# Layer-norm output of an adaLN + attention + FFN block: transposed and scaled by chunks of features instead of tiles of tokens, with a new opening order and a new issue order on every engine

## The chip, the cores and the metric

The kernel runs on one core of one Trainium2 chip. Its time is the device time of one execution in microseconds (us). An engine is one of PE (TensorE: matmuls and transposes), ACT (ScalarE), DVE (VectorE) and POOL (GpSimd); SP (SyncE) issues nearly all DMAs. Each engine runs its own instructions strictly in the order in which they were written, and waits at an instruction until its operands are there.

## The reference

```python
x = A_x                                     # 2048 tokens x 512 features
mod = (silu(c) @ w_mod).reshape(1, 6, 1, 512)   # sa, ca, ga, sb, cb, gb
h = layernorm(x) * (1 + ca) + sa
x = x + ga * A(h)      # q, k, v = h @ wq, h @ wk, h @ wv; 32 heads of 16;
                       # 4 segments of 512 tokens: masked softmax inside a segment,
                       # plus a memory (phi(k)^T v, summed over earlier segments); then @ wo
h = layernorm(x) * (1 + cb) + sb
x = x + gb * (relu(h @ w1 + b1) ** 2 @ w2 + b2)  # 1792 hidden features
```

All in float32. Matrices are 512 features wide, so four 128-row chunks.

## The kernel before, in words

Products of float32 accuracy are made of three products of rounded operands (type `fp32r`): every operand is split into a high half (`hi`, a cast on ACT) and a low half (`lo`, value minus `hi`, a subtraction on DVE or POOL), and hi*hi + hi*lo + lo*hi are summed.

The attention part works on four segments `s` of 512 tokens, each in four units `u = 4s + cc` of eight heads. What the change touches is the way from `x` to the projections of a segment:

- `load_x` brings four tiles `xt` of 128 tokens x 512 features; `ln_stats`, `ln_rstd` and `ln_apply` normalise them (DVE and POOL).
- `ln_transposed` turns one tile on PE (`ln_turn`, four 128x128 transposes into one PSUM bank `blnq`, L610). Each quarter of the bank is one chunk `k` of 128 features, and it has its own scale and bias (`modc`), so `ln_affine` (L616 on ACT, L618 on DVE) applies them in pieces of 128x128: in segment 0 two pieces on ACT and two on DVE for each tile, later four on ACT. `ln_split` (L623) then casts the tile into `HT[:, 0]` and writes the low half into `HT[:, 1]`.
- `HT` is one buffer, 128 features x (hi, lo) x 4 chunks x 512 tokens. `qk(u)` (Q and K of a unit) and `vproj(s)` (V of the segment) read all of it; both wait for all four tiles (`HTN[s]`), and a tile of the next segment waits for every user of the segment before (`HUSE[s - 1]`). The sum over the four chunks is made on half-height arrays, first the upper and lower 64 rows one way (turn 0), then crossed (turn 1), with a tiny ACT instruction (`fence`, L767) between. Unit 0 is the exception: full-height matmuls (L785 to L787) on two halves of 256 tokens.
- `qk` ends with the halves of Q and K in `sg`, and 12 DMAs (`fill`, L845) spread them into the slots `ST` of the scores. `clear` (L717) sets the unused rows of `ST` once from `pad`, six DMAs of 256 KB.
- `a_quad` computes scores (`ba`, L900) of which DVE takes the row maxima (L905, 512 of them with an accumulator read each); `b_quad` computes them again, shifted by the maxima, exponentiates on ACT (`pt`, L1073), masks on POOL (L1060), multiplies with V (`bpv`, L1115).

At the start the scale and bias themselves must be made: `silu(c)` (`crow`, `cs`), two products with `wmod` (`bmod`, L567, for `ca` and `sa`), a copy `t`, and a turn into columns (`bmodc`, L589). Meanwhile the weights are split: `split_w` casts on ACT (L701) and subtracts on POOL (L705; one piece on DVE). `N_WARM` products of the identity with itself (`bwarm`, L539), of which each is two instructions in the trace, fill PE before the first real work.

After the attention come the output projection (`wo_tile`) and the FFN (`bh` L1485, `bpf` L1547 to L1549).

The order on every engine is written out by hand: `ORDER` holds for each engine a list of node numbers, which a planner (`Plan.run`) follows; nodes not in a list follow by priority. The planner assigns buffers; waits come from the real dependences.

## Time and profile before

| | us |
|---|---|
| median of 3 runs (lowest, highest) | 761.86 (759.72, 762.55) |
| the profiled execution: time, span | 762.53, 760.8 |
| busy in the span: PE, DVE, ACT, POOL | 749.1, 604.0, 414.3, 300.7 |
| first real projection (`bqk`, unit 0) starts | 23.74 |
| first score matmul (`ba`) starts | 40.30 |
| first FFN matmul (`bh`), about | 443.1 |

The span is the time from the first to the last recorded event on the core; the execution's time is 1.7 us longer. The granted clock of PE is 0.997 over the span. A busy PE in such a profile can also be a PE between two matmuls, since their ends are modelled, so PE's work is read from how matmuls follow each other.

### The profile page before, as it was taken

What the parts mean: (1) busy time and instruction counts of PE and PEld (TensorE: products, weight loads), DVE (VectorE), ACT (ScalarE), POOL (GpSimd) and SP (SyncE); (2) the same over time, 40 slices, a digit from 0 to 9 for tenths busy, and PEclk for the clock granted to TensorE, in tenths of its full rate; (3) what the DMA queues carried; (4) which work ended last, traced back from release to release, by engine and by line L of the source; (5) the groups of instructions that cost most, each with busy time, mean ns of one, the idle gap of its engine ahead of it and who ended that gap; (6) DMA issues with size and microseconds to landing.
All of it is one profiled execution on the core that took longest, in us unless ns stands there. A gap on an engine that the chain in (4) does not pass through costs nothing.

```text
span 760.8 us, 18140 instructions
## 1 busy us (share of the span) xinstructions
PE 749.1 (98%) x6649; PEld 608.1 (80%) x6649; DVE 604.0 (79%) x1815; ACT 414.3 (54%) x937; POOL 300.7 (40%) x368
## 2 busy tenths in 40 slices
PE   9999999999999999999999999999999999999997
PEld 8987677666787768876666689998999898988986
DVE  5788889999899899999999877868866764666543
ACT  2668777898867987678665844546112321221110
POOL 5676657667677695544241632251010020000000
PEclk9999999999999999999999999999999999999999
DMA  9787574544564345458733157653555345656521
GB/s 308 217 266 223 151 209 126 143 137 120 171 192 100 86 118 156 132 143 247 230 95 127 31 180 273 233 201 140 194 192 210 128 163 208 220 172 217 194 98 69
DMA packets 61058, 129.66 MB, mean 170 GB/s; under 512 B 8613, under 2 KB 23977, under 8 KB 59178
## 3 DMA queue, kind: packets, MB, share of 16 engines
q1 hardware_dynamic: 60818, 128.37, 53.4%
q8 instruction: 53, 0.87, 0.5%
q14 instruction: 35, 0.29, 0.1%
q10 hardware_dynamic: 152, 0.13, 0.1%
HBM read 81.29 MB, written 20.19 MB: 133 GB/s over the span
## 4 chain that ended last, share of the span: by engine, by line
PE 88%; DMA 4%; DVE 2%; ACT 2%; issue 1%; POOL 1%; SPq 1%; DVEq 0%; ACTq 0%; POOLq 0%
PE bh L1485 18%; PE bqk L793 9%; PE bpv L1115 8%; PE bpf L1548 7%; PE bpf L1547 7%; PE bpf L1549 7%; PE bv L866 6%; PE bpb L1056 6%; PE ba L900 6%; PE bwop L1217 2%; PE bwarm L539 2%; PE bwop L1218 2%; PE bwop L1219 2%; PE blnq L610 2%; ACT pt L1073 1%
## 5 line engine op out<-in xcount | busy, mean ns | idle before, releaser
L905 DVE CUSTOM_DVE_ANT_0 ba<-ba,msk 128x384 f32<-128x384 f32 (+3 forms) x512 | 244.4, 511 | 21.0 <-PE ba L900 11.9
L1073 ACT ACTIVATE pt<-bpb 128x512 f32<-128x512 f32 x320 | 171.1, 611 | 28.4 <-PE bpb L1056 25.9
L1060 POOL TENSOR_SCALAR_AFFINE_SELECT pt<-pt 128x512 f32<-128x512 f32 x128 | 80.0, 646 | 91.8 <-ACT pt L1073 70.9
L793 PE MATMUL bqk<-HT,WQK 64*128 64x512 f32 x720 | 106.5, 398 | 0.1
L1056 PE MATMUL bpb<-ST 64*128 64x256 f32 (+2 forms) x512 | 80.2, 349 | 1.7 <-ACT oraw L1139 0.9
L1115 PE MATMUL bpv<-pt,VT 128*32 128x512 f32 (+3 forms) x1024 | 80.8, 440 | 0.7 <-POOL pt L1060 0.2
L793 PEld LDWEIGHTS bqk<-HT,WQK 64*128 64x128 f32 x720 | 74.6, 185 | 8.0 <-issue 1.2
L900 PE MATMUL ba<-ST 63*128 63x256 f32 (+2 forms) x512 | 79.5, 344 | 1.0 <-ACT pt L1073 0.7
L905 DVE DVE_READ_ACCUMULATOR2_ANT mx<- 128x1 f32 x512 | 72.3, 141 | 0.1
L900 PEld LDWEIGHTS ba<-ST 63*128 63x128 f32 x512 | 54.9, 186 | 21.7 <-ACT pt L1073 4.7
L1056 PEld LDWEIGHTS bpb<-ST 64*128 64x128 f32 x512 | 53.9, 186 | 19.4 <-issue 4.5
L1529 ACT CAST ST<-xx 128x512 fp32r<-128x512 f32 x41 | 25.2, 620 | 74.3 <-DVE xx L1521 60.6
L1485 PEld LDWEIGHTS bh<-ST 128*128 128x128 f32 x420 | 56.5, 190 | 3.6
L1485 PE MATMUL bh<-ST 128*128 128x256 f32 x420 | 58.9, 282 | 0.0
L1485 PE MATMUL bh<-ST,w 128*128 128x256 f32 x420 | 58.2, 282 | 0.0
L1485 PEld LDWEIGHTS bh<-ST,w 128*128 128x128 f32 x420 | 55.4, 190 | 2.6
L866 PE MATMUL bv<-WVO,HT 64*128 64x512 f32 x384 | 55.5, 395 | 0.0
L1115 PEld LDWEIGHTS bpv<-pt,VT 128*32 128x32 f32 x1024 | 27.8, 109 | 32.2 <-issue 25.1
L745 POOL TENSOR_TENSOR X1L<-X1L 128x512 fp32r<-128x512 f32 (+1 forms) x28 | 32.1, 1147 | 45.3 <-ACT X1L L744 45.1
L1547 PE MATMUL bpf<-w,ST 128*128 128x512 f32 x124 | 48.9, 395 | 0.0
L1548 PE MATMUL bpf<-w,ST 128*128 128x512 f32 x124 | 48.9, 395 | 0.0
L1549 PE MATMUL bpf<-w,ST 128*128 128x512 f32 x124 | 48.5, 391 | 0.0
(208 smaller groups left out, 1531.9 us busy)
## 6 DMA issues: line engine op xcount, KB each, us to landing
ST<-w1d SPq DMA_DIRECT2D x14, 1792.0 KB
w<-w1d SPq DMA_DIRECT2D x14, 1792.0 KB
ST<-sg SPq DMA_DIRECT2D x192, 128.0 KB
w1d<-X1L SPq DMA_DIRECT2D x21, 512.0 KB
xt<-in_A_x SPq DMA_DIRECT2D x16, 256.0 KB
wm<-in_w_mod SPq DMA_DIRECT2D x16, 256.0 KB
xw<-in_A_x SPq DMA_DIRECT2D x16, 256.0 KB
X1L<-in_B_w SPq DMA_DIRECT2D x7, 512.0 KB
```

Of the source, the lines that this page charges most:

```text
L793: nc.tensor.matmul(bank(banks[w]), W3(w, k, x, cols.start, cols.stop)[r], HT[r, y, k], start=turn == k == i == 0, stop=turn == 1 and k == ...
L866: nc.tensor.matmul(bank(banks[t]), HT[r, x, k, (t2 + t) * P:(t2 + t + 1) * P], WVO[r, k, y], start=turn == k == i == 0, stop=turn == 1 and ...
L900: nc.tensor.matmul(dst[:, c0:c0 + n], ST[b:b + 63, 0, sl, qt * P:(qt + 1) * P], ST[b:b + 63, 1, sl, :n], start=True, stop=True)
L905: nc.vector.tensor_tensor_reduce(i, i, msk[:, 512 - n:], scale=1.0, scalar=-3e38, op0=ALU.add, op1=ALU.max, accum_out=o)
L1056: nc.tensor.matmul(dst, ST[b:b + 64, 1, sl, kb * P:(kb + 1) * P], ST[b:b + 64, 0, sl, q0:512], start=True, stop=True)
L1060: nc.gpsimd.affine_select(out=ap, in_=ap, pattern=[[0, ap.shape[1]], [1, P]], compare_op=ALU.is_ge, fill=0.0, base=0, channel_multiplier=-1)
L1073: ns = [op("ACT", 0.49, lambda j=j: nc.scalar.activation(buf("PPP"[n], pt)[:, i + j], bank(keys[j]), AF.Exp, scale=0.25), pr[slot] + 0.01 ...
L1115: nc.tensor.matmul(bank(o)[32 * hq:32 * hq + 32, q0:q0 + src.shape[1]], v[:, a:a + 32], src, start=start, stop=stop, tile_position=(0, 32 ...
L1485: nc.tensor.matmul(pb(i), A[:, x, kk], B[:, y, kk], start=kk == j == 0, stop=kk == 1 and j == 2)
L1547: nc.tensor.matmul(q, rh, wh, start=(i == 0), stop=False)
L1548: nc.tensor.matmul(q, rh, wl, start=False, stop=False)
L1549: nc.tensor.matmul(q, rl, wh, start=False, stop=(i == NF - 1))
```

## The change

- `ln_chunk` takes the place of `ln_transposed`: for each chunk `k` of features the four tiles are turned into one bank, so that a bank holds one chunk of all 512 tokens, and one instruction of 128x512 applies the scale and bias (in segment 0 chunks 0 and 2 on ACT, 1 and 3 on DVE; later all on ACT). The cast and the subtraction are per chunk too. All four tiles must be normalised before the first transpose.
- `qk` and `vproj` wait for the chunk that each step reads (`HTK`), not for the whole of `HT`, and a chunk of the next segment waits for the last readers of that chunk (`HKUSE`). `chunk` lets the direction alternate, so that the chunk that is free first is filled first and read first.
- Unit 0 is no longer done in two halves of 256 tokens: 24 matmuls of 128x512 in place of 48 of 128x256.
- `N_WARM` is 40 in place of 70.
- `ORDER` is new throughout, on all five engines. Instructions that are neither fillers nor of the way above are the same in kind and number: ACT has 14 instructions of 128x512 for `lnf` in place of 56 of 128x128, DVE 2 in place of 8.

```diff
@@ -31,7 +31,7 @@
-N_WARM = 70
+N_WARM = 40
...
@@ -55,169 +55,168 @@
 ORDER = {
     "PE": """
-8-40 105 111 41 3 42-44 94 86 96 45 88 46-48 117 49 123 50-72 290-291 73-74 292 75-76 293 77 280-282 294 283-284 295
...
+8-24 3 25-35 56 36-39 58 64 78 82 40 66 90 41-42 86 43-47 252 246-247 253 248 254 249 255 401-404 291-292 406 293 407
...
@@ -609,33 +608,26 @@
-    def ln_affine(eng, f, q, sc, bi):
...
-    def ln_split(dst, t, f, low):
...
-    def ln_transposed(s, t, src, dst, pool, sc, bi, pr, after, put, wait=(), low="DVE", kind="#D"):
-
-        b = ("lnq", sc, s, t)
-        f = ("lnf", sc, s, t)
-        n = pe("F", 0.357, lambda: ln_turn(bank(b), src()), pr, after=after, get=[(kind, b)] + ([(pool, f)] if pool != "xr" else []),
-               put=put)
-        if low == "POOL":
-            af = [op("ACT", 1.38, lambda: ln_affine("av", buf(pool, f), bank(b), sc, bi), pr + 0.01, after=[n, *MODC[sc]], put=[b])]
+    def ln_chunk(s, k, pr, applied, wait):
+
+        b, f = ("lnq", s, k), ("lnf", s, k)
+        keys = [("xt", 4 * s + t) for t in range(4)]
+
+        def turn():
+            for t in range(4):
+                nc.tensor.transpose(bank(b)[:, t * P:(t + 1) * P], TL[keys[t]][:, k * P:(k + 1) * P], ident)
+        n = pe("F", 0.357, turn, pr, after=applied, get=[("#D" if s else "#A", b), ("oraw", f)], put=keys)
+        sc, bi = modc[:, CA, k:k + 1], modc[:, SA, k:k + 1]
+        if s or k % 2 == 0:
+            n = act(512, lambda: nc.scalar.activation(buf("oraw", f), bank(b), AF.Identity, scale=sc, bias=bi), pr + 0.01,
+                    after=[n, *MODC[CA]], put=[b])
         else:
-            af = [op("ACT", 0.69, lambda: ln_affine("a", buf(pool, f), bank(b), sc, bi), pr + 0.01, after=[n, *MODC[sc]], put=[b]),
-                  None]
-            af[1] = op("DVE", 0.64, lambda: ln_affine("v", buf(pool, f), bank(b), sc, bi), pr + 0.01, after=[af[0]], put=[b])
-        h = act(512, lambda: ln_split(dst(), t, TL[f], low)[0](), pr + 0.02, sbuf=True, after=[*af, *wait], put=[f])
-        l = op(low, 1.24 if low == "POOL" else 0.6, lambda: ln_split(dst(), t, TL[f], low)[1](), pr + 0.03, after=[h], put=[f], lock=True)
+            n = dve(512, lambda: nc.vector.tensor_scalar(buf("oraw", f), bank(b), sc, bi, op0=ALU.mult, op1=ALU.add), pr + 0.01,
+                    after=[n, *MODC[CA]], put=[b])
+        eng, e = (nc.gpsimd, "POOL") if s else (nc.vector, "DVE")
+        h = act(512, lambda: nc.scalar.copy(HT[:, 0, k], TL[f]), pr + 0.02, sbuf=True, after=[n, *wait], put=[f])
+        l = op(e, 1.24 if s else 0.6, lambda: eng.tensor_tensor(HT[:, 1, k], TL[f], HT[:, 0, k].bitcast(F32), op=ALU.subtract), pr + 0.03,
+               after=[h], put=[f], lock=True)
         return [h, l]
@@ -655,6 +647,11 @@
+    HTK, HKUSE = {}, {s: [[] for _ in range(KD)] for s in range(-1, NS)}
+
+    def chunk(s, turn, i):
+
@@ -668,13 +665,13 @@
-        HTN[s] = []
-        for t in range(4):
-            g = 4 * s + t
-            a = op("DVE", 0.48, lambda t=t, g=g: ln_apply(TL["xt", g], TL["xt", g], TL[mv][:, t]), p_turn[t] - 0.1,
-                   after=[r[t // n]], put=[mv, ("xt", g)], lock=True)
-            HTN[s] += ln_transposed(s, t, lambda g=g: TL["xt", g], lambda: HT, ("phi0", "phi1", "phi1", "oraw")[t] if s == 0 else "oraw", CA, SA, p_turn[t], [a],
-                                    [("xt", g)], HUSE[s - 1], "POOL" if s else "DVE", "#D" if s else "#A")
+        ap = [op("DVE", 0.48, lambda g=g, t=t: ln_apply(TL["xt", g], TL["xt", g], TL[mv][:, t]), p_turn[t] - 0.1,
+                 after=[r[t // n]], put=[mv, ("xt", g)], lock=True) for t, g in enumerate(range(4 * s, 4 * s + 4))]
+        HTK[s] = {}
+        for i in range(KD):
+            k = chunk(s, 0, i)
+            HTK[s][k] = ln_chunk(s, k, p_turn[i], ap, HKUSE[s - 1][k])
+        HTN[s] = [q for k in range(KD) for q in HTK[s][k]]
@@ -779,49 +776,44 @@
-        def mm(w, k, c):
-            p = bank(banks[w])
+        def mm(w, k):
             wh, wl = W3(w, k, 0, cols.start, cols.stop), W3(w, k, 1, cols.start, cols.stop)
-            nc.tensor.matmul(p[:, c], wh, HT[:, 0, k, c], start=(k == 0), stop=False)
-            nc.tensor.matmul(p[:, c], wh, HT[:, 1, k, c], start=False, stop=False)
-            nc.tensor.matmul(p[:, c], wl, HT[:, 0, k, c], start=False, stop=(k == KD - 1))
-
-        def half(turn, k):
+            for x, y, i in ((wh, 0, 0), (wh, 1, 1), (wl, 0, 2)):
+                nc.tensor.matmul(bank(banks[w]), x, HT[:, y, k], start=k == i == 0, stop=k == KD - 1 and i == 2)
+
+        def half(turn, k, first, last):
             for i, (x, y) in enumerate(((0, 0), (0, 1), (1, 0))):
                 for j in (1, 0) if turn else (0, 1):
                     w, r = j ^ turn, slice(64 * j, 64 * j + 64)
-                    nc.tensor.matmul(bank(banks[w]), W3(w, k, x, cols.start, cols.stop)[r], HT[r, y, k], start=turn == k == i == 0,
-                                     stop=turn == 1 and k == 0 and i == 2)
+                    nc.tensor.matmul(bank(banks[w]), W3(w, k, x, cols.start, cols.stop)[r], HT[r, y, k], start=first and i == 0,
+                                     stop=last and i == 2)
         done = {}
         if u:
             n = None
             for turn in (0, 1):
-                for k in range(KD):
-                    if turn and not k:
-                        n = fence(HT[64:65, 0, KD - 1, :1], pr[0] + 0.01, n)
-                    n = pe("R", 0.697, lambda turn=turn, k=k: half(turn, KD - 1 - k if turn else k), pr[turn] + 0.002 * k,
-                           after=[n] if n else [*HTN[s], *(z for w in (0, 1) for z in (WN[w, cc] if s == 0 else []))],
-                           get=() if turn or k else [("#D", b) for b in banks])
-                    if k == 0:
+                for i in range(KD):
+                    k = chunk(s, turn, i)
+                    if turn and not i:
+                        n = fence(HT[64:65, 0, k, :1], pr[0] + 0.01, n)
+                    n = pe("R", 0.697, lambda turn=turn, k=k, i=i: half(turn, k, turn == i == 0, turn == 1 and i == KD - 1), pr[turn] + 0.002 * i,
+                           after=[n, *(HTK[s][k] if not turn else ()),
+                                  *(z for w in (0, 1) for z in (WN[w, cc] if s == turn == i == 0 else []))],
+                           get=() if turn or i else [("#D", b) for b in banks])
+                    if i == 0:
                         HUSE[s].append(n)
+                    if turn:
+                        HKUSE[s][k].append(n)
                 HUSE[s].append(n)
             done[0] = done[1] = n
         for w in (0, 1):
             b = banks[w]
-            ends = []
-            for i in range(0 if u else 2):
-                c = slice(i * L // 2, (i + 1) * L // 2)
-                ht = HTN[s][4 * i:4 * i + 4]
-                n = None
-                for k in range(KD):
-                    n = pe("F", 0.35, lambda w=w, k=k, c=c: mm(w, k, c), pr[w] + 0.002 * k + 0.2 * i,
-                           after=[n] if k else [*ht, *(WN[w, cc] if s == 0 else []), *ends, *([] if u or i or w else [n_w0])], get=() if k or i else [("#D", b)])
-                    if k == 0:
-                        HUSE[s].append(n)
+            for k in range(0 if u else KD):
+                n = done[w] = pe("F", 0.697, lambda w=w, k=k: mm(w, k), pr[w] + 0.002 * k,
+                                 after=[done.get(w), *HTK[0][k], *(WN[w, cc] if k == 0 else []), *([] if k or w else [n_w0])],
+                                 get=() if k else [("#D", b)])
                 HUSE[s].append(n)
-                ends.append(n)
-                done[w] = n
+                HKUSE[s][k].append(n)
@@ -873,12 +865,16 @@
             n = None
             for turn in (0, 1):
-                for k in range(KD):
-                    if turn and not k:
-                        n = fence(WVO[64:65, KD - 1, 0, :1], pr[t2] + 0.01, n)
-                    n = pe("R", 0.697, lambda turn=turn, k=k, mm=mm: mm(turn, KD - 1 - k if turn else k), pr[t2 + turn] + 0.002 * k,
-                           after=[n] if n else [*HTN[s], *([z for c_ in range(4) for z in WN[2, c_]] if s == 0 else [])],
-                           get=() if turn or k else [("#D", b) for b in banks])
+                for i in range(KD):
+                    k = chunk(s, turn, i)
+                    if turn and not i:
+                        n = fence(WVO[64:65, k, 0, :1], pr[t2] + 0.01, n)
+                    n = pe("R", 0.697, lambda turn=turn, k=k, i=i, mm=mm: mm(turn, k, turn == i == 0, turn == 1 and i == KD - 1), pr[t2 + turn] + 0.002 * i,
+                           after=[n, *(HTK[s][k] if not turn else ()),
+                                  *([z for c_ in range(4) for z in WN[2, c_]] if s == turn == i == 0 else [])],
+                           get=() if turn or i else [("#D", b) for b in banks])
+                    if turn:
+                        HKUSE[s][k].append(n)
```

Three places of the order, before and after. PE from its first instruction to unit 0's first projection, before:

```order
L539 MATMUL bwarm<-ident 128x128 x33
L610 MATMUL blnq<-ident,xt 128x128 x8
L539 MATMUL bwarm<-ident 128x128
L529 MATMUL bcs<-ident,crow 128x4
L539 MATMUL bwarm<-ident 128x128 x3
L567 MATMUL bmod<-wmod,cs 32x512 x8
L589 MATMUL bmodc<-selc,t 128x1 x4
...
L610 MATMUL blnq<-ident,xt 128x128 x4
L539 MATMUL bwarm<-ident 128x128 x23
L785 MATMUL bqk<-HT,WQK 128x256
```

and in the change:

```order
L538 MATMUL bwarm<-ident 128x128 x17
L528 MATMUL bcs<-ident,crow 128x4
L538 MATMUL bwarm<-ident 128x128 x11
L566 MATMUL bmod<-wmod,cs 32x512 x4
L538 MATMUL bwarm<-ident 128x128 x4
L588 MATMUL bmodc<-selc,t 128x1 x4
L566 MATMUL bmod<-wmod,cs 32x512 x4
L618 MATMUL blnq<-ident,xt 128x128 x8
...
L618 MATMUL blnq<-ident,xt 128x128 x4
L538 MATMUL bwarm<-ident 128x128 x5
L782 MATMUL bqk<-HT,WQK 128x512 x24
```

The product for `ca` now stands by itself ahead of that for `sa`, the transposes stand behind both, and 5 fillers in place of 23 stand ahead of the first projection. In both versions fillers stand between some of the rows; before, they also stand inside unit 0's projections.

SP's DMAs from the start, before:

```order
L648 DMA xt<-in_A_x 128x512 x4
L552 DMA wmod<-in_w_mod 128x512 x8
L691 DMA w<-in_A_wk 128x4x128
L691 DMA w<-in_A_wk 128x4x384
L691 DMA X1L<-in_A_wq 128x4x128
L691 DMA X1L<-in_A_wq 128x4x384
L691 DMA w<-in_A_wv 128x4x128
L717 DMA ST<-pad 32x4x512 x4
L691 DMA w<-in_A_wv 128x4x384
```

and in the change:

```order
L551 DMA wmod<-in_w_mod 128x512
L640 DMA xt<-in_A_x 128x512 x3
L551 DMA wmod<-in_w_mod 128x512 x3
L640 DMA xt<-in_A_x 128x512
L551 DMA wmod<-in_w_mod 128x512 x4
L688 DMA X1L<-in_A_wq 128x4x128
L688 DMA w<-in_A_wk 128x4x128
L688 DMA w<-in_A_wk 128x4x384
L688 DMA w<-in_A_wv 128x4x128
L688 DMA X1L<-in_A_wq 128x4x384
L688 DMA w<-in_A_wv 128x4x384
L714 DMA ST<-pad 32x4x512 x2
```

The first pieces of `wq` and `wk` are ahead of the rest of the weights, and four of the six `pad` DMAs have moved behind the first fills: two stand behind 17 fills, two behind 31.

ACT where `HT` passes to segment 2 (with the buffers' numbers), before:

```order
L616 ACTIVATE lnf_2934<-blnq_2913,modc_79 128x128 x4
L1008 COPY pk_2958<-bpkt_2941 128x4x64
L1008 COPY pk_2958<-bpkt_2939 128x4x64
L744 CAST X1L_67<-X1L_67 128x512
L1073 ACTIVATE pt_2975<-bpb_2964 128x512
L1073 ACTIVATE pt_2975<-bpb_2965 128x512
L616 ACTIVATE lnf_2987<-blnq_2980,modc_79 128x128 x4
```

and in the change:

```order
L1069 ACTIVATE pt_2464<-bpb_2528 128x512
L622 ACTIVATE lnf_2564<-blnq_2552,modc_79 128x512
L622 ACTIVATE lnf_2573<-blnq_2566,modc_79 128x512
L622 ACTIVATE lnf_2582<-blnq_2558,modc_79 128x512
L764 CAST HT_65<-HT_65 1x1
L1004 COPY pk_2613<-bpkt_2595 128x4x64
L741 CAST X1L_67<-X1L_67 128x512
```

Three instructions of 128x512, for three chunks, stand together where two tiles' eight of 128x128 stood apart, around two exponentials (`pt`); the fourth chunk follows later.

305 lines of the change are left out of this document (147 added, 158 removed), and 16 rows, old and new, of the table ORDER.

## Prediction

> **What bounds the kernel now.** I read the page first, then the windows by stage, the timeline of the opening, and at last the waits. The page gives the totals:
>
> ```profile
> span 760.8 us, 18140 instructions
> PE 749.1 (98%) x6649; PEld 608.1 (80%) x6649; DVE 604.0 (79%) x1815; ACT 414.3 (54%) x937; POOL 300.7 (40%) x368
> ```
>
> PE at 98% says little by itself, since fillers count as busy. The windows tell the stages apart (busy us of PE, PEld, DVE, ACT, POOL, then clock, DMA share, GB/s): the attention from the first score to the first FFN matmul, the FFN, and the last stretch ahead of the first score.
>
> ```profile
> 41.30:443.10 401.80, 396.84 (x4365) 291.80 (x4364) 367.53 (x1345) 304.59 (x721) 238.65 (x296) 1.00 0.53 151
> 443.10:757.00 313.90, 312.86 (x1961) 280.68 (x1959) 210.92 (x421) 90.02 (x176) 39.20 (x32) 1.00 0.52 183
> 30.80:40.30 9.50, 9.50 (x81) 7.67 (x80) 7.13 (x16) 3.60 (x8) 5.71 (x7) 1.00 0.67 186
> ```
>
> In the attention DVE works 367.5 of 401.8 us (91%): it is the engine that sets the pace, with PE close behind. In the FFN PE works 312.9 of 313.9 and DVE only 210.9. Ahead of the first score DVE works 7.1 of 9.5 us, and before that PE waits, as the next rows show. So the kernel is a start of 41 us, a stretch at DVE's pace, and a stretch at PE's. What is saved ahead of the first score moves everything behind it. The start on PE:
>
> ```profile
> 1.90 9.01 PE L539 MATMUL bwarm<-ident 128*128 128x128 f32 x66 [1.90 <-POOL ident masks.py:199]
> 10.75 1.04 PE L610 MATMUL blnq<-ident,xt 128*128 128x128 f32 x8
> 12.96 1.92 PE L567 MATMUL bmod<-wmod,cs 128*32 128x512 f32 x16
> 16.03 0.95 PE L589 MATMUL bmodc<-selc,t 128*128 128x1 f32 x8
> 18.69 5.30 PE L539 MATMUL bwarm<-ident 128*128 128x128 f32 x46
> 23.74 0.37 PE L785 MATMUL bqk<-HT,WQK 128*128 128x256 f32 x1
> 30.77 3.01 PE L793 MATMUL bqk<-HT,WQK 64*128 64x512 f32 x24
> 39.28 1.09 PE L610 MATMUL blnq<-ident,xt 128*128 128x128 f32 x8
> 40.30 0.51 PE L900 MATMUL ba<-ST 63*128 63x256 f32 x4
> ```
>
> From 18.69 to 23.74 PE does nothing but fillers: it waits for the chain scale and bias, `lnf`, `HT`. That chain on ACT and DVE:
>
> ```profile
> 17.66 2.19 ACT L616 ACTIVATE lnf<-blnq,modc 128x128 f32<-128x128 f32 x6
> 21.17 1.14 ACT L623 CAST HT<-lnf 128x512 fp32r<-128x512 f32 x2
> 17.02 0.16 DVE L591 TENSOR_SCALAR modc<-bmodc 128x4 f32<-128x4 f32 x1 [0.96 <-PE bmodc L589]
> 21.91 1.29 DVE L623 TENSOR_TENSOR HT<-lnf,HT 128x512 fp32r<-128x512 f32 x2
> 24.57 2.39 DVE L623 TENSOR_TENSOR HT<-lnf,HT 128x512 fp32r<-128x512 f32 x2 [0.74 <-ACT HT L623]
> 25.14 1.27 POOL L705 TENSOR_TENSOR WQK<-w,WQK 128x512 fp32r<-128x512 f32 x1 [4.81 <-ACT WQK L701]
> ```
>
> The scale and bias are there at 17.18, the first low halves at 23.2, and the last at 26.96: ten us for four tiles.
>
> **The opening, part by part.** When do the loads land? The transfer rates in slices of 1 us, and one wait that a landing ended:
>
> ```profile
> GB/s 0 18 230 350 299 289 352 369 363 361 373 357 370 364 343 342 369 343 359 331 257 277 312 246 96 115 375 402 406 262 37 0 33 172 203 129 110 346 386 281
> 16.62 0.62 ACT L701 CAST WQK<-X1L 128x512 fp32r<-128x512 f32 x1 [1.01 <-DMA X1L<-in_A_wq]
> ```
>
> Twelve loads of 256 KB (262 KB of 1000 bytes; `x`, then both `wmod`) are 3146 KB, which the rates reach at 11.4; `bmod` starts at 12.96. Up to the first piece of `wq` it is 4456 KB, reached at 15.05; ACT starts at 16.62. Both lag by 1.56 us, so I take landing = bytes moved + 1.56. In the change the last tile of `x` is load 8 (2097 KB, 8.5 + 1.56 = 10.1), `ca`'s weights are complete with load 7 (9.4), `sa`'s with load 12 as before (12.96), the first piece of `wq` follows (13.7).
>
> The tokens become the later branch: the fourth tile must have its statistics, `rstd`, and all four their scaling ahead of any transpose. The nearest rows:
>
> ```profile
> 9.95 0.69 DVE L597 BATCH_NORM_STATS2 bs<-xt 128x6 f32<-128x512 f32 x1
> 10.94 0.22 POOL L602 TENSOR_SCALAR mv<-mv 128x2 f32<-128x2 f32 x1 [1.95 <-DVE mv L598]
> 11.24 0.71 POOL L603 TENSOR_TENSOR mv<-mv,nhalf 128x2 f32<-128x2 f32 x1
> 11.99 1.00 DVE L606 TENSOR_SCALAR xt<-xt,mv 128x512 f32<-128x512 f32 x2 [1.14 <-POOL mv L603]
> ```
>
> From the start of the statistics to the first scaling is 2.04 us: 10.1 + 2.0 = 12.1. Four scalings at 0.46 with one `modc` (0.16) between end at 14.2. Eight transposes take 0.87 (10.75 to the next row at 11.62), a filler 0.22: `bmodc` starts at 15.3, `modc` is there 1.15 later (16.03 to 17.18): 16.45, against 17.18. Now four chunks, not four tiles with four pieces each. ACT does chunk 0 and its cast (0.6 each, ending 17.75), DVE chunks 1 and 3 in the meantime (0.61 each, to 17.8), then the low half of chunk 0 (0.7): 18.5. Unit 0 starts at about **18.55, against 23.74**. Chunk 1 follows in time; chunk 2 stands last on ACT and DVE (cast 19.95, low half 20.7), so the third step waits 0.8. Four steps a matrix at 0.70 (three matmuls at twice the 0.116 of L785 to L787), 24 matmuls in all: unit 0 ends at 24.95, unit 1 starts at **25.05 against 30.77**. Its weights allow that: of the second cast pieces POOL makes `wk`, `wq` and three of `wv` at 1.27 each from about 21.1, so `wq` is done at 23.6 and V's last at 27.7; PE reaches V at 25.05 + 24 x 0.116 = 27.85.
>
> Up to the first score PE does 66 matmuls of the half-height kind (72 in 8.5 us before, 0.118 each): 7.8, so `ba` at **32.85 against 40.30**. But 6 of those matmuls and 8 transposes (1.7 us) are only moved behind it, so PE gains 5.75. The fills allow it narrowly:
>
> ```profile
> 31.49 2.65 SPq L845 DMA_DIRECT2D ST<-sg  x4
> 54.98 2.81 DMA ST<-sg
> 36.24 1.46 DVE L606 TENSOR_SCALAR xt<-xt,mv 128x512 f32<-128x512 f32 x3 [0.71 <-POOL mv L603]
> 40.69 0.69 DVE L829 TENSOR_TENSOR sg<-bqk,sg 128x512 fp32r<-128x512 f32 x1 [0.95 <-ACT sg L827]
> ```
>
> The cast of K ends at 25.8, six fills at 0.65 from there and one wait are issued by 29.7, and landing takes 2.8: 32.5. DVE starts its maxima at 33.3 against 41.30, but three scalings (1.46) and two `sg` (1.38) that were done ahead of them now come behind: 8.0 - 2.9 = 5.1. DVE sets the pace afterwards, so the opening is worth **-5.1**. Bounds: -5.75 (PE's count) to -2.3, if the low halves meet POOL as in the row at 24.57 (two in 2.39, against 1.29 without POOL: +1.1) and one window of PE is slow (+1.7, below). I take POOL to be idle there, since its next operands stand on ACT behind the casts of `HT`. [...]
>
> **The attention behind it.** What its instructions cost DVE does not change. ACT loses work: 48 pieces make way for 12.
>
> ```profile
> L616 ACT ACTIVATE lnf<-blnq,modc 128x128 f32<-128x128 f32 x48 | 18.0, 473 | 0.2
> 63.43 4.03 ACT L1073 ACTIVATE pt<-bpb 128x512 f32<-128x512 f32 x8
> 159.80:184.80 25.00, 23.60 (x318) 13.91 (x314) 23.55 (x97) 23.68 (x58) 20.70 (x22) 1.00 0.50 128
> 259.10:277.70 18.60, 18.11 (x238) 10.71 (x234) 17.43 (x71) 17.99 (x42) 14.19 (x16) 1.00 0.24 63
> 67.40:82.60 15.20, 14.62 (x174) 8.28 (x172) 12.49 (x50) 13.20 (x33) 10.06 (x12) 0.89 0.57 164
> ```
>
> A 128x512 from PSUM takes 0.50 in a row of eight, so 12 cost 6.0 and ACT is relieved of 12 us, in and ahead of the three stretches in which `HT` passes on. There ACT works 23.7 of 25, 18.0 of 18.6 and 13.2 of 15.2 us. But DVE is nearly as full: its idle time in the three is 1.45, 1.2 and 2.7, so no more than 5.3 can be had; I take half, -2.6. The fine waits per chunk belong to the same time and are not counted again: the order starts units 4, 8 and 12 at the same count of score matmuls as before (68, 206, 330), so they are not used to start a segment earlier. PE changes between full, half-height and quarter-width matmuls 149 times instead of 157; at 0.15 each (eight transposes from 39.28 take 0.87, and `ba` follows at 40.30) that is 1.2 at most, and 0 where DVE is the limit: -0.4. On the other side a new order can stall elsewhere:
>
> ```profile
> DVE ba L905 <- PE ba L900: 11.9, 25, 2.2
> ```
>
> DVE's longest wait for scores is 2.2; one more of these at each passing of `HT` would cost 6.6. So this part is **-3.0**, bounds -6.5 and +6.6. The FFN keeps its 1176 `bh` and 672 `bpf` on a saturated PE: 0.
>
> Sum: 762.53 (the profiled execution) - 5.1 - 3.0 = 754.4. The median of the runs shown lies 0.67 below that execution, so **753.8**.
>
> **The rivals.** (1) *The relief of ACT is worth nothing*, since DVE has no slack to give: 762.53 - 5.1 - 0.67 = 756.8. For it: DVE's 91%. Against it: waits for `pt` do reach PE there. (2) *The opening gives only its lower bound*: -2.3 and nothing behind, 759.6. Fewer fillers stand ahead of the projections, and PE's clock can drop:
>
> ```profile
> 73.10:76.50 3.40, 2.82 (x50) 2.16 (x52) 2.90 (x13) 3.19 (x7) 2.22 (x2) 1.00 0.78 270
> 76.50:79.90 3.40, 3.40 (x44) 1.23 (x29) 2.63 (x9) 2.75 (x8) 2.46 (x5) 0.50 0.43 157
> ```
>
> After a stretch of 3.4 us in which PE idled 0.58, the next 3.4 us ran at half the clock; full of matmuls that costs 1.7. My estimates leave PE idle about 0.6 between 11.8 and 14.2 too (waiting for `t`, for `sa`'s weights and for the scaled tokens). [...] (3) *Slower: late fills.* Four `pad` DMAs move among the fills of units 1 and 2. Before, four of them held SP for this long:
>
> ```profile
> 12.65 5.28 SPq L717 DMA_DIRECT2D ST<-pad  x4
> SPq L845 <- ACT sg L827: 5.6, 1, 5.6
> ```
>
> and their 1.05 MB take 3.6 us of the queue at 289 GB/s, an ordinary slice of the row above. It decides only where unit 1's fills are the last thing that a score waits for, and SP has no slack; then 5.3 + 3.6 outweigh 5.1, PE starves, and a window at half clock (the row at 76.50) adds 1.7: 762.53 - 5.1 + 5.3 + 3.6 + 1.7 - 0.67 = 767.4. Against it: SP itself waited 5.6 us for `sg` ahead of the first fill, so it is not full from the start. (4) *The order is better throughout*: the full 6.5 behind the opening, and 5.75 in it: 749.6.
>
> **How the numbers follow.** Forecast 0.48, (1) 0.20, (2) 0.14, (3) 0.08, (4) 0.10. The range **749.5 to 760.5** holds the first three and half of the fourth. No change means within 0.5% (3.8 us, 758.05 to 765.7), about what a measurement can tell. Faster: the forecast, (4), and most of (1) and a little of (2): 0.76; same 0.16; slower 0.08.
>
> **What would show it.** In the new profile: unit 0's first matmul at 18 to 19.5, unit 1 at 25 to 26, `ba` at 32.5 to 33.5; its last low halves without a neighbour on POOL (0.6 apart); DVE's idle time between first score and first `bh` about 32 instead of 34.3; first `bh` 7 to 9 us earlier; FFN 314 long. I am wrong if the last tile of `x` lands after 10.1, if a fill is what the first scores wait for, if a window at half clock stands in the opening, or if DVE idles more in the attention than before.

## The result and the profile after

The changed kernel takes 756.1 us (median of 4 runs, 755.5 to 756.2) against 761.7 us before (4 runs): a ratio of 0.9928, interval 0.9908 to 0.9948. Run a second time beside other kernels it gave 0.9936 (0.9916 to 0.9956). The forecast was 753.8 us, range 749.5 to 760.5. The profiled execution of the change took 755.5 us (span 753.8), that of before 762.5, so the traces differ by 7.0 us where the medians differ by 4.7 to 5.6: the one of before was a long one, the one of after a short one.

The page's totals of the changed kernel:

```profile
span 753.8 us, 17858 instructions
PE 741.7 (98%) x6565; PEld 596.6 (79%) x6565; DVE 603.4 (80%) x1809; ACT 403.2 (53%) x895; POOL 303.2 (40%) x368
```

The windows that answer to those shown of before (attention, FFN, last stretch ahead of the first score; busy us of PE, PEld, DVE, ACT, POOL, then clock, DMA share, GB/s):

```profile
33.40:437.00 403.60, 397.67 (x4388) 289.44 (x4385) 368.10 (x1350) 299.97 (x691) 238.98 (x296) 0.99 0.54 154
437.00:750.00 313.00, 312.91 (x1961) 281.07 (x1959) 213.69 (x421) 87.77 (x175) 41.97 (x32) 1.00 0.53 186
25.00:33.40 8.40, 7.98 (x67) 6.16 (x68) 6.88 (x14) 3.92 (x9) 8.32 (x8) 1.00 0.49 116
```

The opening is shorter and the attention behind it is not: 403.6 us from the first score (33.40) to the first FFN matmul, where before took 402.7. (The 401.8 shown of before starts at 41.30, which is the first maximum; its first score stands at 40.30.) ACT works 300.0 us in it for 305.6 from that first score on, DVE 368.1 for 368.0. The opening on PE, in the timeline:

```profile
11.09 1.06 PE L566 MATMUL bmod<-wmod,cs 128*32 128x512 f32 x8
13.96 1.06 PE L566 MATMUL bmod<-wmod,cs 128*32 128x512 f32 x8
16.11 0.95 PE L588 MATMUL bmodc<-selc,t 128*128 128x1 f32 x8
19.31 5.70 PE L782 MATMUL bqk<-HT,WQK 128*128 128x512 f32 x24
24.95 3.04 PE L788 MATMUL bqk<-HT,WQK 64*128 64x512 f32 x24
33.40 0.70 PE L896 MATMUL ba<-ST 63*128 63x256 f32 x8
```

and its chain on ACT and DVE:

```profile
17.30 0.78 ACT L622 ACTIVATE lnf<-blnq,modc 128x512 f32<-128x512 f32 x1 [1.02 <-DVE modc L590]
18.11 1.66 ACT L628 CAST HT<-lnf 128x512 fp32r<-128x512 f32 x3
10.47 0.70 DVE L596 BATCH_NORM_STATS2 bs<-xt 128x6 f32<-128x512 f32 x1 [0.93 <-DMA xt<-in_A_x]
17.30 1.53 DVE L625 TENSOR_SCALAR lnf<-blnq,modc 128x512 f32<-128x512 f32 x2
18.76 1.90 DVE L629 TENSOR_TENSOR HT<-lnf,HT 128x512 fp32r<-128x512 f32 x3
```

Unit 0 starts at 19.31 (before 23.74), unit 1 at 24.95 (30.77), the first score at 33.40 (40.30). How this lead fares behind is first read by placing the same matmul, or the maximum of the same count, in both traces (us from the span's start):

| place | before | after | difference |
|---|---|---|---|
| unit 1, first matmul | 30.77 | 24.95 | -5.8 |
| first maximum (unit 0) | 41.30 | 33.86 | -7.4 |
| 33rd maximum (32 a unit) | 59.34 | 58.64 | -0.7 |
| 65th maximum | 82.53 | 78.38 | -4.2 |
| 97th maximum | 106.07 | 106.17 | +0.1 |
| unit 8, first matmul | 184.84 | 181.47 | -3.4 |
| unit 12, first matmul | 277.71 | 271.89 | -5.8 |
| first `bh` | 443.00 | 437.03 | -6.0 |
| last matmul, end | 756.95 | 749.91 | -7.0 |

**By this count nothing is left of the lead at 106 us, and 6 us are gained behind it.** But the count compares two orders: the two kernels issue their maxima in a different sequence (in 231 of the 512 places the widths differ), so a maximum of the same count is not the same work. A kernel that has the change's order and not its opening is needed to say what became of the lead; experiments 1 and 2 have it. The stretch in windows, before and then after:

```profile
41.30:106.00 64.70, 63.94 (x730) 50.39 (x732) 57.58 (x226) 49.42 (x126) 45.72 (x48) 0.97 0.70 204
106.00:443.10 337.10, 332.90 (x3639) 241.40 (x3632) 309.95 (x1120) 255.17 (x595) 192.93 (x248) 1.00 0.50 141
```

```profile
34.00:106.00 72.00, 67.67 (x770) 49.47 (x770) 61.97 (x238) 50.62 (x120) 47.33 (x49) 0.95 0.76 225
106.00:437.00 331.00, 329.40 (x3614) 239.38 (x3607) 305.54 (x1112) 249.35 (x571) 191.40 (x246) 1.00 0.49 138
```

Up to 106 us DVE has 4.4 us more work (62.0 for 57.6) and some 3 us more idle time, PE idles 4.3 us for 0.8, and the clock is lower. Behind 106 DVE has 4.4 us less to do: more than half of what looks lost up to 106 is work that the new order takes earlier. One stall of the first stretch, in the timelines of ACT, PE and DVE:

```profile
50.76 0.62 ACT L741 CAST X1L<-X1L 128x512 fp32r<-128x512 f32 x1 [2.86 <-DMA w1d<-X1L]
52.42 0.50 PE L1052 MATMUL bpb<-ST 64*128 64x512 f32 x1 [1.62 <-ACT phi L828]
56.65 0.57 DVE L901 CUSTOM_DVE_ANT_0 ba<-ba,msk 128x384 f32<-128x384 f32 x1 [3.28 <-PE ba L896]
```

ACT stands at a cast that prepares weights for the FFN until an earlier write has landed; `e` and `phi` of unit 2 are behind it in ACT's order, PE waits for `phi`, and DVE for PE. Later PE's clock drops:

```profile
68.40:71.80 3.40, 2.55 (x21) 1.88 (x19) 3.06 (x10) 3.40 (x8) 3.40 (x3) 1.00 0.84 201
71.80:75.20 3.40, 2.93 (x18) 1.60 (x21) 2.22 (x9) 2.45 (x7) 2.27 (x3) 0.50 0.67 222
75.20:78.60 3.40, 3.40 (x28) 1.76 (x24) 2.86 (x13) 2.10 (x6) 1.95 (x3) 0.50 0.02 5
```

That is 6.8 us at half clock, where before had 3.4 (at 76.5).

### The profile page after: what moved, and what is told of

Same layout as the page of the kernel before. It is cut to its first block, busy times and chain, and to the rows that moved or that the text cites. A ratio compares the mean times of both kernels' runs of the same rounds, so it can differ in the third digit from the quotient of the medians.

```text
span 753.8 us, 17858 instructions
## 1 busy us (share of the span) xinstructions
PE 741.7 (98%) x6565; PEld 596.6 (79%) x6565; DVE 603.4 (80%) x1809; ACT 403.2 (53%) x895; POOL 303.2 (40%) x368
## 4 chain that ended last, share of the span: by engine, by line
PE 86%; DVE 4%; DMA 3%; ACT 3%; POOL 2%; issue 2%; SPq 0%; ACTq 0%; DVEq 0%; POOLq 0%
PE bh L1481 18%; PE bpv L1111 8%; PE bqk L788 8%; PE bpf L1544 7%; PE bpf L1543 7%; PE bpf L1545 7%; PE bpb L1052 6%; PE ba L896 6%; PE bv L858 5%; PE bwop L1213 2%; PE bwop L1215 2%; PE bwop L1214 2%; DVE ba L901 2%; PE bwarm L538 1%; ACT pt L1069 1%
## 5 line engine op out<-in xcount | busy, mean ns | idle before, releaser
L901 DVE CUSTOM_DVE_ANT_0 ba<-ba,msk 128x256 f32<-128x256 f32 (+3 forms) x512 | 244.4, 511 | 24.9 <-PE ba L896 15.4
L1069 ACT ACTIVATE pt<-bpb 128x512 f32<-128x512 f32 x320 | 173.1, 608 | 43.1 <-PE bpb L1052 38.4
L788 PE MATMUL bqk<-HT,WQK 64*128 64x512 f32 x720 | 104.9, 397 | 0.0
L1052 PE MATMUL bpb<-ST 64*128 64x256 f32 (+2 forms) x512 | 83.6, 353 | 1.9 <-ACT phi L828 1.6
L896 PE MATMUL ba<-ST 63*128 63x256 f32 (+2 forms) x512 | 78.6, 345 | 2.9 <-ACT pt L1069 1.0
L788 PEld LDWEIGHTS bqk<-HT,WQK 64*128 64x128 f32 x720 | 71.7, 185 | 8.6 <-issue 1.4
L896 PEld LDWEIGHTS ba<-ST 63*128 63x128 f32 x512 | 53.1, 188 | 21.8 <-ACT pt L1069 5.9
L1312 POOL TENSOR_TENSOR tt<-h2raw 128x512 f32<-128x512 f32 x8 | 10.8, 1352 | 99.7 <-ACT h2raw L1277 35.3
L1543 PE MATMUL bpf<-w,ST 128*128 128x512 f32 x116 | 45.8, 395 | 0.0
L1544 PE MATMUL bpf<-w,ST 128*128 128x512 f32 x116 | 45.7, 394 | 0.0
```

The source lines that it names most:

```text
L788: nc.tensor.matmul(bank(banks[w]), W3(w, k, x, cols.start, cols.stop)[r], HT[r, y, k], start=first and i == 0, stop=last and i == 2)
L896: nc.tensor.matmul(dst[:, c0:c0 + n], ST[b:b + 63, 0, sl, qt * P:(qt + 1) * P], ST[b:b + 63, 1, sl, :n], start=True, stop=True)
L901: nc.vector.tensor_tensor_reduce(i, i, msk[:, 512 - n:], scale=1.0, scalar=-3e38, op0=ALU.add, op1=ALU.max, accum_out=o)
L1052: nc.tensor.matmul(dst, ST[b:b + 64, 1, sl, kb * P:(kb + 1) * P], ST[b:b + 64, 0, sl, q0:512], start=True, stop=True)
L1069: ns = [op("ACT", 0.49, lambda j=j: nc.scalar.activation(buf("PPP"[n], pt)[:, i + j], bank(keys[j]), AF.Exp, scale=0.25), pr[slot] + 0.01 ...
L1543: nc.tensor.matmul(q, rh, wh, start=(i == 0), stop=False)
```

## The experiments

All ratios are to the kernel before on the same chip, with 95% intervals. "ORDER" stands for the lists that set each engine's order.

**1. The opening alone, and the rest alone.** The change was cut in two at the first score. In the first kernel the new opening stands ahead of tiles and the old order; in the second the old opening stands ahead of chunks and the new order. The lists are spliced, so each has a seam that was not tuned.

```diff
+        if s == 0:          # opening alone; the rest alone has "if s:"
             for i in range(KD):
                 k = chunk(s, 0, i)
                 HTK[s][k] = ln_chunk(s, k, p_turn[i], ap, HKUSE[s - 1][k])
+        else: for t in range(4): HTN[s] += ln_transposed(s, t, ...)
 ORDER: up to the first score of the one kernel, behind it of the other
```

> The new opening alone: segment 0 by chunks, 40 fillers and the new order up to the first score, behind it the turning by tiles (four pieces on ACT) and the old order, which has room for neither the moved scalings nor the new fills. By the prediction's split (opening 5.1 us, the rest 3.0 us) it takes 5.1 us off: 756.6 us, a ratio of 0.993, first score at 33 to 34 us. If the relief of ACT is worth nothing (rival 1) and the opening is all of it: 755 to 756.5 us, 0.991 to 0.993. If the start is given back behind it in stalls up to 106 us, as the trace of the change hints, and the gain of segments 1 to 3 comes from the chunks and the new order: 759.5 to 761 us, 0.997 to 0.999, with the first maxima 7 us earlier and those of segment 1 no earlier than before.

> The rest alone: the old opening (tiles, 70 fillers, old order up to the first score), behind it segments 1 to 3 by chunks with one affine for four pieces, waits per chunk and the new order. By the prediction's split it takes 3.0 us off: 758.7 us, 0.996. If the relief of ACT is worth nothing: 761.7 us, 1.000 (760.5 to 763). If the gain of segments 1 to 3 in the trace of the change (4 to 6 us) belongs to the chunks and the order: 756.5 to 757.7 us, 0.994.

Measured: the opening alone 1.003 (1.0007 to 1.0052), 2.3 us *longer* than before. The rest alone 0.9968 (0.9945 to 0.9991), 2.4 us shorter. The parts add up to nothing, both together bring 4.9 us. In the first kernel the first score stands at 32.93, 7.4 us ahead of before, but the first maximum at 36.78 is only 4.5 ahead, since the old order has the scalings and `sg` in front of it; the 33rd maximum stands at 60.07, 0.7 behind. (This kernel issues its maxima in the sequence of before, so here the counts can be compared.) Between them, in its timelines of SP, DVE, PE, DVE and ACT:

```profile
34.33 4.88 SPq L755 DMA_DIRECT2D ST<-pad  x4
36.78 0.42 DVE L942 CUSTOM_DVE_ANT_0 ba<-ba,msk 128x256 f32<-128x256 f32 x1
45.40 0.64 PE L937 MATMUL ba<-ST 63*128 63x256 f32 x4 [3.47 <-DMA ST<-sg]
46.18 0.43 DVE L942 CUSTOM_DVE_ANT_0 ba<-ba,msk 128x256 f32<-128x256 f32 x1 [3.69 <-PE ba L937]
46.63 0.41 ACT L782 CAST X1L<-X1L 128x256 fp32r<-128x256 f32 x1 [5.55 <-DMA w1d<-X1L]
```

Four `pad` DMAs hold SP for 4.9 us in the middle of unit 0's fills; then PE waits 3.5 us for a fill, and ACT 5.6 us for a `w1d` write that was issued behind them. That is rival 3 at work.

**2. The pads out of the fills.** In the opening alone, and in the change itself, the four pads are issued at 22 to 27 us, in a gap of SP ahead of the first fill.

```diff
 ORDER "SP": ... ge-load
+  pad pad pad pad
   fills of unit 0 ...
-  pad pad          (opening alone: among unit 0's; change: among unit 1's)
   fills ...
-  pad pad          (change: among unit 2's)
```

> The new opening alone, as in the run of that name, but with the four pad DMAs that stood there at 34.3 to 39.2 us among the fills of unit 0 issued ahead of the first fill, at 20.8 us. There PE waited 3.5 us for a fill at 41.9, DVE 3.7 us, and half a window of clock was lost. If those four DMAs are why the opening alone brings nothing: that wait goes, the first maxima stay 6 to 7 us ahead at unit 1, and the time is 3 to 6 us shorter than the opening alone, ratio to before 0.995 to 0.999. If the whole stream of transfers of 26 to 62 us (85% busy in every kernel so far) is the bound, the wait only moves to the next fills: 1.001 to 1.003.

> The change with the four late pad DMAs (1.05 MB, 2.6 us of SP) issued ahead of the first fill, where SP stands idle from 20.5 to 25.7 us, and not among the fills of units 1 and 2. If late fills are a price of the change (rival 3): units 1 to 3 come up to 2.6 us earlier, 1 to 2.6 us shorter than the change, ratio 0.990 to 0.992. If SP has slack there: as the change, 0.993 to 0.994. If the pads now delay the first fills, on which the first scores wait: the first score after 34 us and 1 to 4 us longer, 0.995 to 0.999.

Measured: the opening alone with early pads 0.9985 (0.9966 to 1.0003), 3.4 us less than without; its unit 3 starts 3.9 us ahead of before, not 0.7 behind, and up to 62 us no score waits for a fill any more. In its trace the first maximum is 3.5 us ahead of before, the 97th 4.5 and the last 2.5. By the ratio 1.1 us reach the end, an amount that its interval does not tell from none. The change with early pads 0.9899 (0.9877 to 0.9922): 754.05 us, about 2.8 us less than the change. DVE's waits for scores between 34 and 108 us, in the change and then with early pads (us in total, times, longest):

```profile
DVE ba L901 <- PE ba L896: 7.1, 6, 3.3
ACT X1L L741 <- DMA w1d<-X1L: 3.6, 3, 2.9
```

```profile
DVE ba L901 <- PE ba L896: 3.3, 5, 1.1
```

The wait of 2.86 us for `w1d` is gone (0.9 us is the longest left): in the change two pads were issued at 43.46, just ahead of that write at 46.35. So the late pads cost the change some 2.8 us (0.5 to 5 by the two intervals); the wait that went with them is that for the write behind them, not one for a fill. The intervals of the two kernels overlap at their edges, so the size is less sure than the sign.

The rest alone, the change and the change with early pads issue all 512 maxima in the same sequence, so that these three show what the opening is worth ahead of one and the same order (us from the span's start):

| place | rest alone | change | change, early pads |
|---|---|---|---|
| first maximum | 41.87 | 33.86 | 35.23 |
| 33rd maximum | 64.02 | 58.64 | 58.27 |
| 97th maximum | 108.98 | 106.17 | 103.94 |
| last maximum | 424.00 | 419.74 | 418.64 |
| first `bh` | 441.29 | 437.03 | 435.91 |
| ratio to before | 0.9968 | 0.9936 | 0.9899 |

From the first to the 97th maximum, in this order:

```profile
41.87:108.98 67.11, 65.15 (x760) 48.32 (x758) 59.68 (x234) 48.37 (x116) 47.17 (x49) 0.97 0.70 208
33.86:106.17 72.31, 67.98 (x776) 49.75 (x776) 62.27 (x241) 50.62 (x120) 47.33 (x49) 0.95 0.76 225
35.23:103.94 68.71, 66.11 (x776) 50.09 (x777) 62.21 (x238) 50.40 (x120) 47.24 (x49) 0.98 0.73 222
```

The change starts 8.0 us ahead of the rest alone and is 2.8 ahead at the 97th maximum: DVE works 2.6 us more in between (three scalings and two `sg`, 2.7 us in its timeline, that now come behind the first maximum) and idles 10.0 us for 7.4. With early pads 6.6 us become 5.0: the same extra work, and only 6.5 us idle. So the lead is not gone. By the ratios the opening is worth 2.4 us ahead of this order, and 5.3 with the pads out of the way; each difference is sure to some 2.5 us either way, since every ratio has an interval of its own and the kernels did not all run on one chip.

**3. The two casts on ACT, moved back.**

```diff
 ORDER "ACT": sg sg
-  X1L
   e phi
+  X1L
   ...
-  X1L
   sg sg
+  X1L
```

> The change with two casts of the weights for the FFN moved back in ACT's order: the one that waited 2.9 us for its buffer's write at 47.9 goes behind e and phi of unit 2, the one that waited 2.4 us for its load at 65.2 behind both sg of unit 3; their halves on POOL and their writes follow by one or two places. If these two waits are where the start was given back: e and phi are there at 49, DVE's idle time of 3.3 us at 53.4 and the windows at half clock behind 71.8 go, and the time is 2 to 4 us shorter than the change, ratio to before 0.988 to 0.991. If the fills and their transfers bound units 1 to 3 anyway, as the transfers at 85% suggest: within 1 us of the change, 0.992 to 0.995, with the idle time of DVE only moved.

> Both repairs of the change together: pads ahead of the first fill and the two casts for the FFN moved back on ACT. Alone the pads took off 2.8 us, the casts 2 us (0 to 3.6). If the two act on different waits: 4 to 5 us shorter than the change, ratio to before 0.986 to 0.988. If both ease the same queue of transfers: no more than the pads alone, 0.989 to 0.991.

Measured: 0.9920 (0.9899 to 0.9940), 754.75 us; with early pads as well 0.9899 (0.9872 to 0.9926), no more than the pads alone. In the timeline of ACT of the first (an execution of 758.24 us, the longest of its six):

```profile
49.86 0.60 ACT L826 ACTIVATE e<-bqk 128x512 f32<-128x512 f32 x1 [0.87 <-DVE sg L821]
53.41 0.62 ACT L741 CAST X1L<-X1L 128x512 fp32r<-128x512 f32 x1 [2.46 <-DMA w1d<-X1L]
```

and among its waits between 34 and 108 us:

```profile
DVE ba L901 <- PE ba L896: 9.2, 7, 5.5
```

`e` and `phi` come on time, but the same cast now holds up `pt`, and DVE waits 9.2 us for scores, not 7.1. In this execution the wait was moved, not removed, which points to the late write and not to the place of the cast; the time is not to be told from that of the change.

**4. The relief of ACT taken back, and DVE loaded by as much.**

```diff
-            n = act(512, lambda: nc.scalar.activation(buf("oraw", f), bank(b), ...))
+            for t in range(4): nc.scalar.activation(buf("oraw", f)[:, c], bank(b)[:, c], ...)   # s > 0
```

```diff
+                for _ in range(2 if s and w == 0 else 1):
                     nc.vector.tensor_tensor(TL[sg][:, 2 * w + 1], bank(b), TL[sg].bitcast(F32)[:, 2 * w], op=ALU.subtract)
```

> The change with the relief of ACT taken back: each of the 12 affines of segments 1 to 3 is four pieces of 128 columns again, with the order untouched. By the rows (0.375 us a piece, 0.71 us for a whole one) ACT works 9.5 us more, just ahead of and in the three turnovers of HT. By the prediction's term half of what DVE idles there comes through: 2 to 3.5 us longer than the change, ratio to before 0.996 to 0.998. If the relief is worth nothing (rival 1): as the change, 0.992 to 0.995. If ACT sets the end there: 7 to 9.5 us longer, 1.002 to 1.006.

> The change with DVE given more work: in each of the 12 units of segments 1 to 3 the first low half of sg is made twice (12 times 0.60 us, 7.2 us in all), the order untouched. If DVE sets the pace of the attention, all of it comes through: 6.5 to 8 us longer than the change, ratio to before 1.002 to 1.004. If PE, ACT and the transfers bound as much of it: 2 to 4 us, 0.996 to 0.999. If nothing hangs on DVE there: 0.993.

Measured: the pieces on ACT 1.0034 (1.0014 to 1.0054), 7.3 us longer than the change; the work on DVE 1.0053 (1.0032 to 1.0073), 7.6 us longer by the medians and 8.9 by the ratios. The affines in the groups of the change, in those of the kernel with pieces, and then two of that kernel's waits between 34 and 437 us:

```profile
L622 ACT ACTIVATE lnf<-blnq,modc 128x512 f32<-128x512 f32 x14 | 10.5, 781 | 2.1 <-DVE modc L590 1.0 <-PE blnq L618 1.0
```

```profile
L625 ACT ACTIVATE lnf<-blnq,modc 128x128 f32<-128x128 f32 x48 | 17.6, 477 | 0.5 <-PE blnq L618 0.4
```

```profile
DVE ba L905 <- PE ba L900: 24.3, 26, 3.5
PEld bpb L1056 <- ACT lnf L625: 4.6, 5, 1.2
```

and `sg` on DVE in the groups of the change, then of the kernel with more work on DVE:

```profile
L821 DVE TENSOR_TENSOR sg<-bqk,sg 128x512 fp32r<-128x512 f32 x32 | 21.3, 686 | 5.3 <-ACT sg L819 4.3 <-POOL mv L601 0.8
```

```profile
L823 DVE TENSOR_TENSOR sg<-bqk,sg 128x512 fp32r<-128x512 f32 x44 | 29.6, 687 | 5.1 <-DMA ge<-in_A_beta 2.6 <-ACT sg L819 1.0 <-POOL mv L601 0.8
```

Without the two affines of the opening (1.6 us) the 12 cost 8.9 us: ACT works 8.7 us more in pieces, and 84% of it come through. DVE works 8.3 us more with the 12 doubled (not the 7.2 of the expectation), and all of it comes through within the noise. In the kernel with pieces DVE waits 24.3 us for scores, where the same row of the change has 15.4, and PE's weight loads wait 4.6 us with `bpb` for a bank that the pieces free late. So an ACT that is 74% busy sets the end there nearly as much as DVE does. The order of these kernels is tuned for the shorter work; a new search might win some of it back, so 7.3 us is, within the noise, an upper bound of what the relief is worth.

**5. The fillers.** In the change, the 11 ahead of the first product with the modulation weights are left out; in the kernel before, the last 30, most of which stand ahead of unit 0.

```diff
-N_WARM = 40      # the change; before: 70 to 40
+N_WARM = 29
```

> The change with the 11 fillers left out that stand between the transposition of the condition and the first product with the modulation weights (22 matmuls, 8.44 to 11.09 us in the change). If they hold up that product, whose weights have landed by 9.4 us in the prediction: scale and bias and with them unit 0 come 0.5 to 1 us earlier, 18.3 to 18.8 us, 0 to 1 us off the time, ratio to before 0.992 to 0.994. If PE's clock hangs on them: a window at half clock between 10 and 17 us, unit 0 at 19.5 to 21 and 0.5 to 2 us longer, 0.994 to 0.997.

> The kernel before with 40 fillers for 70: the 30 last ones, which stand ahead of the first projection while PE waits for the low halves, are left out, nothing else. If they only keep the clock: PE idles some 3 us of the 5 from 18.7 to 23.7, one or two windows of 3.4 us at half clock fall on unit 0, the first score comes 1.7 to 3 us later and the time is 1.5 to 3 us longer, ratio 1.002 to 1.004. If the fillers count for nothing: unit 0 at 23.7, same clock, 1.000.

Measured: 0.9934 (0.9907 to 0.9962), the change's own time, and 1.0017 (0.9995 to 1.0038), not to be told from nothing. In PE's timeline of the change with fewer:

```profile
8.01 1.98 PE L566 MATMUL bmod<-wmod,cs 128*32 128x512 f32 x8 [0.25 <-ACT cs L530]
17.78 5.72 PE L782 MATMUL bqk<-HT,WQK 128*128 128x512 f32 x24
```

The fillers do hold up that product: with them it starts at 10.34 to 11.62 us in five executions of this opening. Unit 0 comes 1.5 us earlier than in the execution shown (0.8 to 2.6 earlier than in the five), at a full clock (1.00 from 6.9 to 24.0 us). The time is that of the change, but two intervals of this width can't tell whether 1.5 us reach the end or not; in the trace the last maximum stands at 419.00, for 419.74 and 420.24 in two executions of the change. In the kernel before with fewer, PE idles 3.2 us (its timeline) and a window at half clock follows (0.50 from 23.6 to 25.3 us; 0.84 is the clock over the stretch 24 to 32 us):

```profile
22.26 0.39 PE L785 MATMUL bqk<-HT,WQK 128*128 128x256 f32 x1 [3.23 <-ACT HT L623]
```

```profile
24.00:32.00 8.00, 8.00 (x59) 7.62 (x60) 4.67 (x7) 6.60 (x14) 6.61 (x5) 0.84 0.53 197
```

Unit 0 still starts earlier (22.26 for 23.74, since no filler stands ahead of it), and unit 1 at 30.48 for 30.77.

**6. An order for late transfers, and the change again.** An order searched for starts behind the opening with slower writes, with early pads; and the change as it is.

```diff
 ORDER: 107 of 879 steps moved on ACT, 185 of 403 on SP, 62 on DVE, 56 on POOL, 17 on PE
```

> The change with the pads ahead of the first fill and an order that was searched on for starts behind the opening, with the writes of split weights assumed 1.5 us slower, so that late transfers cost less (on ACT 107 of 879 steps are moved, on SP 185 of 403, on PE 17). If the stalls of the change come from its order having no slack for late transfers: 4 to 8 us shorter than the change, ratio 0.983 to 0.988. If the transfers bound it whatever the order: as the pads alone, 0.989 to 0.991.

> The change as it is, once more, for the same chip and for what varies between executions: ratio 0.991 to 0.995. If the two windows at half clock at 71.8 to 78.6 us come from the late e, phi and sg of units 0 to 3, they stand there again, within a window's length; if they are chance, they do not. The FFN is 1 us shorter than before only if the wait for a weight at 699 us in the execution of before was chance.

Measured: 0.9974 (0.9949 to 0.9998), 5.7 us worse than early pads with the order of the change. Between 34 and 108 us DVE waits 5.0 us for scores there (7.1 in the change), and ACT 8.6 us for loads of FFN weights (4.5). Why this order is worse is open. The change again: 0.9936; first score at 32.64, first `bh` at 437.53; two windows at half clock are there again, but only one where the first pair stood (73 to 77 us), the other at 53 to 56. One near 72 to 80 stands in the traces of before, of the opening alone, of the rest alone and of the change with early pads too, so that one window there is no mark of the change.

## Why the prediction was right or wrong

The total lay in the range, and 4.7 to 5.6 us came off where 8.1 were forecast (753.8 forecast, 756.1 and 756.8 measured). The profiled executions differ by -7.4 up to the first maximum, +1.5 from there to the first `bh`, and -1.1 behind: the forecast had -8.0, -0.1 (2.9 of moved work and -3.0) and 0.

- **The opening by itself: right.** Landing of the last tile of `x`: 10.47 for 10.1, late by the prediction's own list of signs, but without harm. Scale and bias: 17.26 for 16.45. Unit 0 at 19.31 for 18.55, unit 1 at 24.95 for 25.05, the first score at 33.40 for 32.85, the first maximum at 33.86 for 33.3. Two small errors: the affine takes 0.78 us (DVE 0.77), not 0.6; 11 fillers held up the first product, which cost unit 0 some 1.5 us (0.8 to 2.6). The low halves ran 0.6 apart (three in 1.90, from 18.76) while POOL did nothing (4.61 us idle ahead of 22.23), as taken.
- **"What is saved ahead of the first score moves everything behind it": not as the change issues its pads. This is the step that failed, in the term of -5.1.** Ahead of one and the same order the opening brought 2.4 us, and 5.3 with the pads ahead of the fills. The sum took the four pads that move behind the first score at nothing and left them to rival 3 with a chance of 0.08, since SP had waited for `sg` before; they cost some 2.8 us, and what waited in the trace was ACT, at a cast whose buffer's write had been issued behind them. The premise that DVE sets the pace held: work added to DVE in segments 1 to 3 came through in full, and with early pads DVE idles 31.6 us from the first maximum to the first `bh` (400.7 us less 369.1 of work) where 32 was forecast, the first `bh` comes 7.1 us earlier than before (7 to 9 forecast), and the median is 754.05. Ahead of the old order the step failed in another way: the opening alone is 2.3 us longer than before, and with early pads at best 1.1 shorter, with a first maximum 3.5 us ahead. Why so little of that arrives is open.
- **The moved DVE work (2.9): right.** Against the rest alone, DVE works 2.6 us more between the first and the 97th maximum. From the first maximum to the first `bh` it works 367.4 us before and 367.7 in the change all the same: the new order takes out as much (the rest alone has 365.9 us there).
- **The attention behind it (-3.0): right in size for the part alone, for partly wrong reasons.** The rest alone brought 2.4 us (0.7 to 4.2). But ACT is relieved of some 9 us, not 12 (12 affines cost 8.9 us, not 6.0), and what DVE idles in the turnovers did not bound the gain: taken back, the relief costs 7.3 us. How the 2.4 us split into relief, waits per chunk and order is not settled.
- **What neither term had: the parts need each other.** The opening alone and the rest alone add up to -0.1 us, together they bring 4.9. Late pads cost the opening alone 3.4 us and the change 2.8, so they don't explain the difference. In the change `bpb` starts at 50.3 us, in the rest alone at 56.9, in the opening alone at 62.4: the new order may be able to spend the lead where the old one can't, and the seams have a price. Neither was measured by itself.
- **The FFN (0): right.** The -1.1 of the traces lies within what varies: the execution of before has one wait of 1.0 us for a weight near 699 us, and over all kernels run, whose FFN is the same work, it took 312.6 to 314.4 us.
- **The rivals.** (1), the relief worth nothing, fell in experiment 4. (2): no window at half clock stood in the opening (the clock is 1.00 up to the first score), but two stood at 71.8 to 78.6, a stretch that the argument had not looked at. (3), late pads, is real at 2.8 us in the change and at 3.4 in the opening alone; the price of 10.6 us was too high. (4) was not seen. DVE idled 35.5 us from the first maximum to the first `bh`, where 32 was forecast and 34.3 stood before, which the prediction itself names as a sign of being wrong; the first `bh` came 6.0 us earlier, not 7 to 9.

The range held since its upper part allowed for a smaller gain, for other reasons than the one that came. Taken in turn, the rest brought 2.4 us of 3.0 and the opening, put ahead of it, 2.4 of 5.1; both fell short.

## What to carry to other kernels

A lead ahead of a stretch arrives in full only if nothing that was done in the time saved is put in the way behind: here transfers of no urgency, moved among urgent ones on one in-order queue, took about half of it (2.8 of 5.3 us). Look at the first 50 us behind the lead by themselves (what stands among the fills, which in-order engine waits for a write), not at the mean of the stage. To see what became of a lead, compare kernels with the same order behind it; markers counted in two different orders showed a lead as lost that was not. Before costing a relief at the idle time that it can fill, add as much work to the engine instead and see how much comes through; here it was 84% on an ACT at 74% and all of it, within the noise, on DVE. Cutting a change in two shows what its sum hides: two halves worth +2.3 and -2.4 us made 4.9 together.

## What the runs showed of the hardware

A 128x512 affine with scale and bias per partition from PSUM took 0.78 us on ACT, where the exponential of the same shape took 0.61 and 0.50 in a row of eight. In the change PE was busy 2.55 of the 3.4 us ahead of 71.8, at a clock of 1.00, and the next 3.4 us ran at half clock; it was busy 2.93 of these, and the next 3.4 us ran at half clock too; it was busy through all of those, and the clock was full again. No share of its time that decides could be read here: it also idled 1.62 us ahead of 52.42, and the clock stayed at 1.00. With one and the same opening, unit 0 started anywhere from 18.56 to 20.39 us in five profiled executions; of the two of the change itself the one with the earlier unit 0 (18.56 for 19.31) took longer (756.7 us for 755.5).
